# Attention products with v stored place by place innermost and summed by one reduction, and a new table of task places

## Chip, cores and metric

The kernel runs on one core of one Trainium2 chip. The metric is the device time of one execution in microseconds. Before the change three runs gave 622.37, 621.45 and 622.18 us; their median is 622.18 us. One more execution was profiled: its time was 621.86 us, and the profile's span (first to last instruction) is 620.1 us, so 1.76 us of that execution lie outside the span.

## What is computed

A token mixes two branches, attention with 32 heads over 8 places that lie 2 apart, and a Mish MLP, by a sigmoid gate:

```python
B, S, D = 1, 2048, 640; H = 32; Dh = 20; W, dil = 8, 2
idx = pos[:, None] - off[None, :]              # off = arange(8) * 2
logits = einsum("bhsd,bhswd->bhsw", q, kg) * scale    # masked where idx < 0
attn = softmax(logits, axis=-1)
o = einsum("bhsw,bhswd->bhsd", attn, vg)
a = o.reshape(B, S, D) @ wo
h = einsum("bsd,df->bsf", x, w1) + b1          # F = 1728
b = einsum("bsf,fd->bsd", h * tanh(softplus(h)), w2)
out = g * a + (1 - g) * b                      # g = sigmoid((x * gate_w).sum(-1))
```

The change touches the line that makes `o`.

## The kernel before

All matrix products run on TensorE (PE) with float32 inputs split into a high and a low part, so that each product is three matmuls (lines 481 to 483, function `mm3`). The split of a tile is made by two other engines: ScalarE (ACT) copies the high part (line 433), and VectorE (DVE) or GpSimd (POOL) subtracts it from the original to get the low part (line 436). The two parts lie in a `pair` tile, which PE reads. PE writes to seven PSUM banks.

The work is a list of tasks: `qkv` products for a quarter of the heads and half of the tokens at a time (eight units), `mlp1` and `quad` for the first MLP layer (a quad makes four blocks from seven products and hands partial sums from one bank to the next by ACT copies, line 927), `mlp2` for the second layer, and `wo_out` for the output product. The order of the products is given by the strings `FRONT` and `BACK`.

Attention itself is done by DVE. For each of the eight units there are four pieces of 2 x 128 tokens. In `scores` one multiplication of q with k for eight places (line 534, 2560 elements per partition) is followed by a reduction over the 20 features of a head (line 537). ACT has put q into the PSUM tile `side` before (line 540, task kind `qs`). In `outputs` the weights go to `side` (line 576), a multiplication with v (line 572) writes `pr` as [2 slots, 8 places, 160 features], and three additions halve the number of places: 8 to 4 (line 582), 4 to 2 (line 583), 2 to 1 into `q` (line 585).

The order of instructions on each engine is made when the program is built, by the class `Plan`: it plays the tasks through with a cost in ns each and takes, for an engine that is free, the task that is first by rank, due time and place in the list. Tasks of engine `ANY` (low parts and sums) go to POOL or DVE. While DVE is in a long instruction (`LARGE`: kinds `qk`, `qk sum`, `pv`), POOL may take a task that ends within it; while DVE is in any other instruction, POOL takes only tasks of rank below zero. Five tables correct single tasks by their number in the list: `MOVED` (place in the list), `HELD_BACK` (ready later), `NEEDED` (due time), `RANKED` (rank) and `ENGINE` (1 is DVE alone, 2 is POOL alone).

```python
LARGE, TOUCH = ("qk", "qk sum", "pv"), ("qk", "w", "pv")
...
if on and busy["DVE"]:
    fit = [t for t in fit if now + t.ns[0] <= quiet + 150 or t.rank < 0]
...
if t.kind in LARGE:
    begun = True
    quiet, gate = now + t.ns, last
```

DMAs of inputs, spills and results are issued by SyncE (SP); the sums of two MLP blocks are made by accumulating DMAs that POOL issues (line 723).

Of the kernel before, what the change touches and what calls it, by code (L numbers as in the profile page):

```python
# [11 lines left out]
OP = mybir.AluOpType  # L12
AX = mybir.AxisListType
# [3 lines left out]
S, D, H, DH, W, F = 2048, 640, 32, 20, 8, 1728  # L17
# [59 lines left out]

MOVED = """18:-4 500:-142 922:197 1244:301 1321:-2 1941:232"""  # L80
HELD_BACK = """110:1256 126:2874 359:1662 387:971 500:2708 581:193 635:839 703:214 822:16218 826:757 828:355 844:2726 848:5943
864:315 922:175 962:1932 963:501 1140:2261 1141:272 1142:308 1160:189 1243:1453 1246:859 1263:2549 1321:1969
1334:1062 1385:130 1756:782 1825:788 1862:478 2377:760 2413:1116 2426:2529"""
NEEDED = """110:-2061 119:-19498 126:21019 581:-1563 635:20514 822:-10954 828:12301 844:-408404 846:-3895 848:56321 931:-884144
937:33210 942:-278 962:3606 963:588 1140:661 1160:-787 1263:-714 1333:-255 1385:1390 1825:-252 1837:-186 2152:1905
2209:-17463 2413:1130 2426:-5153"""
RANKED = """80:0.25 822:-15.75 826:-1.25 828:-0.25 844:-10.25 848:-15.75 931:-119.25 937:-14 943:-1 1332:-1 1355:-1 1368:-1
1385:0.75 1753:-1 1837:0.25 1862:-1 2377:-0.25 2426:1"""
ENGINE = """119:2 846:2 1753:1 1756:1 1803:1 2128:2 2182:2 2252:1"""


class Plan:
# [36 lines left out]
    def run(self):  # L129
# [8 lines left out]
        touched = copied = None  # L138
        moved, held, needed, ranked, engine = map(table, (MOVED, HELD_BACK, NEEDED, RANKED, ENGINE))
        for i, t in enumerate(self.tasks):  # L140
# [144 lines left out]
def kernel(ctx: ExitStack, tc: tile.TileContext, x, wq, wo, w1, b1, w2, out):  # L285
    nc = tc.nc
    scale = DH ** -0.5
    V, G, A = nc.vector, nc.gpsimd, nc.scalar
# [112 lines left out]
    pw = side[:, :2 * W * HQ].rearrange("p (s w h) -> p s w h", w=W, h=HQ)  # L401
    qs = side[:, 2 * W * HQ:2 * W * HQ + 2 * QF].rearrange("p (s f) -> p s f", f=QF)
    pr = at.tile([128, 2, W, QF], F32, name="pr")
    mx = at.tile([128, 8, HQ], F32, name="mx")
    sm = at.tile([128, 8, HQ], F32, name="sm")

# [97 lines left out]
    def window(kv, s0, which):  # L504
        a = kv[:, s0:s0 + 9, which, :]
        return bass.AP(tensor=a.tensor, offset=a.offset, ap=[list(a.ap[0]), [ROW, 2], [ROW, W], [1, QF]])
# [7 lines left out]
    def attention(u, P, hq, ready, gates):  # L514


        kv, q = KV[UNIT[u]], Q[UNIT[u]]

        def turn_of(h, k):
            return LATER + 0.008 * (h + k / 7)  # L520

        def chain(rank):

            prev = [None]

            def step(eng, ns, fn, after=(), **k):
                prev[0] = add(eng, ns, fn, [prev[0]] + list(after), rank=rank if prev[0] is None else LATER - 0.5, **k)
                return prev[0]

            return step  # L530
# [30 lines left out]
        def shares(a, rank, after):  # L561
            h = slice(a, a + 4)
            step = chain(rank)
            step("DVE", 415, lambda: V.tensor_reduce(sm[:, h], lg[:, h], op=OP.add, axis=AX.X), after)
            step("DVE", 390, lambda: V.reciprocal(sm[:, h], sm[:, h]))
            return step("DVE", 230, lambda: V.tensor_tensor(sm[:, h], sm[:, h], gate[:, P, h, None].to_broadcast([128, 4, HQ]), op=OP.mult), gates)

        def outputs(s0, rank, after):
            def mul():
                vw = window(kv, s0, 1)  # L570
                vw = bass.AP(tensor=vw.tensor, offset=vw.offset, ap=[list(d) for d in vw.ap[:3]] + [[DH, HQ], [1, DH]])
                return V.tensor_tensor(pr.rearrange("p s w (h d) -> p s w h d", d=DH), vw,  # L572
                                       pw[:, :, :, :, None].to_broadcast([128, 2, W, HQ, DH]), op=OP.mult)

            def weights():
                return V.tensor_tensor(pw.rearrange("p s w h -> p s h w"), lg[:, s0:s0 + 2],  # L576
                                       sm[:, s0:s0 + 2, :, None].to_broadcast([128, 2, HQ, W]), op=OP.mult)

            step = chain(rank)
            step("DVE", 300, weights, after, kind="w")  # L580
            step("DVE", 2820, mul, kind="pv")
            step("DVE", 1495, lambda: V.tensor_tensor(pr[:, :, 0:4], pr[:, :, 0:4], pr[:, :, 4:8], op=OP.add))  # L582
            step("DVE", 855, lambda: V.tensor_tensor(pr[:, :, 0:2], pr[:, :, 0:2], pr[:, :, 2:4], op=OP.add))  # L583

            return step("DVE", 525, lambda: V.tensor_tensor(q[:, s0:s0 + 2], pr[:, :, 0], pr[:, :, 1], op=OP.add))

        def out(s0, rank, after):
            ot = plan.buf("ot", lambda: at.tile([128, QF // 32, 4, 32], F32, name="ot"))
# [8 lines left out]
        for i, a in enumerate((4, 0)):  # L597
            h = 2 * u + i
            t1 = scores(a + 2, turn_of(h - 1, 0), [shared_out.get(h - 2), prev])
            t2 = scores(a, turn_of(h - 1, 3), [t1])  # L600
            e = softmax(a, turn_of(h - 1, 6), [bounded(a, a + 4, [t1, t2])])
            w = shares(a, turn_of(h, 1), [e, shared_out.get(h - 2)])

            o = outputs(a + 2, turn_of(h, 2), [w, shared_out.get(h - 1)])
            o = outputs(a, turn_of(h, 4), [o])
            att_end[u] = out(a, turn_of(h, 5), [o])
            shared_out[h] = o
            prev = t2
# [859 lines left out]
```

## Time and profile before

| | busy us | share of span | instructions |
|---|---|---|---|
| PE matmuls | 614.4 | 99% | 2717 |
| DVE | 561.0 | 90% | 582 |
| ACT | 385.5 | 62% | 851 |
| POOL | 256.7 | 41% | 249 |

| | us |
|---|---|
| median of three runs | 622.18 |
| the profiled execution | 621.86 |
| its span | 620.1 |

A group of the profile names line, engine, operation and tiles with their shapes; `x32` is its count, then come the busy time, the mean ns of one, and the idle time of the engine just ahead of them. In a timeline a row gives the start, the length, the engine, the line, and in brackets how long the engine was idle ahead of it and what released it. Matmul records overlap, because matmuls are pipelined: a wait of PE is seen best in the distance between two starts.

### The profile page before, as it was taken

To read this page: it belongs to the slowest core of one execution; us is meant where nothing else is said; L and a number is where in the kernel's file an instruction comes from. 1 tells how busy PE (TensorE), PEld (TensorE's weight loads), DVE (VectorE), ACT (ScalarE), POOL (GpSimd) and SP (SyncE) were. 2 spreads that over 40 slices of the span, in tenths; PEclk is the share of its full clock that TensorE was granted. 3 is DMA by queue.
4 is the path that set the end of the run, shared out by engine and by line. 5 is a ranking of instruction groups with operands and counts; after the bars stand their busy time and mean duration, and the time that the engine had idled before them with its cause. 6 is when DMAs were issued, how large, how long until landed. Compare 5 with 4: busy or idle time off the path is not lost.

```text
span 620.1 us, 8931 instructions
## 1 busy us (share of the span) xinstructions
PE 614.4 (99%) x2717; PEld 509.3 (82%) x2717; DVE 561.0 (90%) x582; ACT 385.5 (62%) x851; POOL 256.7 (41%) x249
## 2 busy tenths in 40 slices
PE   9999999999999999999999999999999999999997
PEld 6888878887888888888888888888888888888885
DVE  5899999999999999999999999999899999999630
ACT  6765765766686677666676553556868356664234
POOL 2763267645464455445355665542013333303000
PEclk9999999999999999999999999999999999999999
DMA  8867289999999599989997999798987686965404
GB/s 308 260 197 209 86 251 267 287 252 243 322 258 283 150 319 298 232 235 271 265 259 212 315 265 263 214 274 287 347 278 255 214 274 215 284 212 175 135 1 170
DMA packets 100608, 149.46 MB, mean 241 GB/s; under 512 B 11456, under 2 KB 47296, under 8 KB 100528
## 3 DMA queue, kind: packets, MB, share of 16 engines
q1 hardware_dynamic: 93456, 136.05, 67.8%
q0 software_dynamic: 7104, 12.85, 13.1%
q8 instruction: 21, 0.34, 0.2%
q14 instruction: 27, 0.22, 0.1%
HBM read 85.61 MB, written 60.69 MB: 236 GB/s over the span
## 4 chain that ended last, share of the span: by engine, by line
PE 83%; DVE 11%; DMA 2%; issue 2%; ACT 1%; SPq 0%; POOL 0%; DVEq 0%; POOLq 0%; ACTq 0%
PE bank L481 27%; PE bank L483 27%; PE bank L482 27%; DVE pr L534 3%; DVE lg L537 2%; DMA raw<-in_x 2%; DVE pr L572 1%; DVE pair L436 1%; DVE pr L582 1%; DVE kvq L436 1%; PE bank L1248 1%; PE bank L1247 1%; DVE raw L780 0%; ACT L735 0%; SPq L442 0%
## 5 line engine op out<-in xcount | busy, mean ns | idle before, releaser
L482 PE MATMUL bank<-pair,pair 128*128 128x512 f32 (+2 forms) x812 | 314.5, 387 | 0.0
L483 PE MATMUL bank<-pair,pair 128*128 128x512 f32 (+2 forms) x812 | 314.4, 387 | 0.0
L481 PE MATMUL bank<-pair,pair 128*128 128x512 f32 (+2 forms) x812 | 314.2, 387 | 0.0
L436 POOL TENSOR_TENSOR pair<-raw,pair 128x512 fp32r<-128x512 f32 (+3 forms) x109 | 138.0, 1279 | 211.5 <-DVE side L576 39.0
L481 PEld LDWEIGHTS bank<-pair,pair 128*128 128x128 f32 x812 | 152.5, 188 | 30.2
L483 PEld LDWEIGHTS bank<-pair,pair 128*128 128x128 f32 x812 | 152.5, 188 | 30.1 <-POOL pair L436 0.2
L482 PEld LDWEIGHTS bank<-pair,pair 128*128 128x128 f32 x812 | 152.4, 188 | 30.1
L433 ACT ACTIVATE pair<-raw 128x512 fp32r<-128x512 f32 (+3 forms) x198 | 116.9, 610 | 32.7 <-DMA raw<-act 13.2
L572 DVE TENSOR_TENSOR pr<-kvq,side 128x2560 f32<-128x2560 f32 x32 | 90.2, 2820 | 1.0
L537 DVE TENSOR_REDUCE lg<-pr 128x128 f32<-128x2560 f32 x32 | 90.2, 2817 | 0.7
L534 DVE TENSOR_TENSOR pr<-kvq,side 128x2560 f32<-128x2560 f32 x32 | 90.0, 2812 | 0.4
L436 DVE TENSOR_TENSOR pair<-raw,pair 128x512 fp32r<-128x512 f32 (+4 forms) x89 | 58.5, 678 | 6.3 <-ACT pair L433 6.3
L633 ACT ACTIVATE kvq<-bank 128x320 f32<-128x320 f32 x64 | 27.9, 436 | 49.0 <-PE bank L483 48.5
L582 DVE TENSOR_TENSOR pr<-pr 128x1280 f32<-128x1280 f32 x32 | 47.7, 1490 | 0.7
L433 ACT ACTIVATE pair<-hb 128x512 fp32r<-128x512 f32 (+2 forms) x40 | 24.7, 618 | 15.3 <-DMA hb<-actt 7.7
L927 ACT ACTIVATE bank<-bank 128x512 f32<-128x512 f32 x36 | 21.0, 584 | 17.8 <-PE bank L483 17.5
L780 POOL TENSOR_TENSOR raw<-raw,raw 128x256 f32<-128x256 f32 (+1 forms) x20 | 20.6, 1034 | 25.7 <-DVE side L576 10.0
L481 PE MATMUL bank<-kvq,pair 128*128 128x512 f32 x72 | 28.3, 392 | 0.3 <-ACT bank L927 0.3
L723 POOL DMA_DIRECT2D actt<-actt x26 | 22.6, 881 | 13.5 <-DVE side L576 6.8
L483 PE MATMUL bank<-kvq,pair 128*128 128x512 f32 x72 | 28.1, 391 | 0.1
L482 PE MATMUL bank<-kvq,pair 128*128 128x512 f32 x72 | 28.0, 390 | 0.0
L583 DVE TENSOR_TENSOR pr<-pr 128x640 f32<-128x640 f32 x32 | 26.3, 823 | 0.8
(126 smaller groups left out, 583.4 us busy)
## 6 DMA issues: line engine op xcount, KB each, us to landing
raw<-in_w SPq DMA_DIRECT2D x34, 256.0 KB, 3.8
raw<-in_wq SPq DMA_DIRECT2D x30, 248.0 KB, 4.2
raw<-in_x SPq DMA_DIRECT2D x29, 256.0 KB, 5.3
raw<-actt SPq DMA_DIRECT2D x29, 256.0 KB, 4.5
actt<-hb SPq DMA_DIRECT2D x28, 256.0 KB, 3.4
act<-z SPq DMA_DIRECT2D x24, 256.0 KB, 4.4
actt<-z SPq DMA_DIRECT2D x24, 256.0 KB, 4.8
raw<-act SPq DMA_DIRECT2D x23, 256.0 KB, 3.9
```

What stands on the lines that cost most here:

```text
L433: a = add("ACT", act_ns(n), lambda: A.activation(hi(), raw(), AF.Copy), after, rank=rank, take=take, hold=hold, kind="hi")
L436: return (V if e == "DVE" else G).tensor_tensor(lo(), raw(), hi().bitcast(F32), op=OP.subtract)
L481: nc.tensor.matmul(ps, ah, bh, start=first, stop=False, skip_group_check=more)
L482: nc.tensor.matmul(ps, ah, bl, start=False, stop=False, skip_group_check=more)
L483: nc.tensor.matmul(ps, al, bh, start=False, stop=last, skip_group_check=more)
L534: return V.tensor_tensor(pr, window(kv, s0, 0), qs[:, :, None, :].to_broadcast([128, 2, W, QF]), op=OP.mult)
L537: return V.tensor_reduce(lg_w[:, s0:s0 + 2], pr.rearrange("p s w (h d) -> p s w h d", d=DH), op=OP.add, axis=AX.X)
L572: return V.tensor_tensor(pr.rearrange("p s w (h d) -> p s w h d", d=DH), vw, pw[:, :, :, :, None].to_broadcast([128, 2, W, HQ, DH]), op=OP ...
L582: step("DVE", 1495, lambda: V.tensor_tensor(pr[:, :, 0:4], pr[:, :, 0:4], pr[:, :, 4:8], op=OP.add))
L583: step("DVE", 855, lambda: V.tensor_tensor(pr[:, :, 0:2], pr[:, :, 0:2], pr[:, :, 2:4], op=OP.add))
L633: a = add("ACT", 330, lambda: A.activation(kv[:, 7 + s], ps.t[:, QF:3 * QF].rearrange("p (a b) -> p a b", a=2), AF.Copy), [done] + before, ...
L723: return add("POOL", 1200, lambda: G.dma_start(out=blk[key][:rows], in_=src(), accum_op=OP.add, max_dma_last_dim=2048), after, rank=-0.5, ...
```

## The change

The multiplication with v writes `pr` as [2 slots, 160 features, 8 places]: the same 2560 products, with the eight places of a feature side by side. One reduction over the innermost eight elements takes the place of the three additions. It carries the task kind `qk sum`, which is in `LARGE`, so that POOL may take tasks while it runs. Two tasks fewer for each of the 32 pieces shift the numbers of the task list, and the five tables are replaced: 173 tasks are named in them. The first line of two tables is shown; the rest is of the same kind.

```diff
-MOVED = """18:-4 500:-142 922:197 1244:301 1321:-2 1941:232"""
+MOVED = """3:-35739 474:-184 642:705 952:23 1073:18 1119:407 1589:110 2347:-102"""
...
-ENGINE = """119:2 846:2 1753:1 1756:1 1803:1 2128:2 2182:2 2252:1"""
+ENGINE = """105:2 609:2 787:2 798:2 804:2 814:2 822:1 824:2 1180:1 1344:2 1387:1 1431:1 1736:1 1765:1 1768:1 1787:1 1938:1
...
     pr = at.tile([128, 2, W, QF], F32, name="pr")
+
+    by_place = pr.rearrange("p s w f -> p (s w f)").rearrange("p (s f w) -> p s f w", s=2, w=W)
...
-                return V.tensor_tensor(pr.rearrange("p s w (h d) -> p s w h d", d=DH), vw,
+                return V.tensor_tensor(by_place.rearrange("p s (h d) w -> p s w h d", d=DH), vw,
                                        pw[:, :, :, :, None].to_broadcast([128, 2, W, HQ, DH]), op=OP.mult)
...
             step("DVE", 2820, mul, kind="pv")
-            step("DVE", 1495, lambda: V.tensor_tensor(pr[:, :, 0:4], pr[:, :, 0:4], pr[:, :, 4:8], op=OP.add))
-            step("DVE", 855, lambda: V.tensor_tensor(pr[:, :, 0:2], pr[:, :, 0:2], pr[:, :, 2:4], op=OP.add))
-
-            return step("DVE", 525, lambda: V.tensor_tensor(q[:, s0:s0 + 2], pr[:, :, 0], pr[:, :, 1], op=OP.add))
+            return step("DVE", 2820, lambda: V.tensor_reduce(q[:, s0:s0 + 2], by_place, op=OP.add, axis=AX.X), kind="qk sum")
```

On DVE the program has 582 instructions before and 474 after: 64 fewer by the reduction (32 pieces, three additions against one reduction), and 44 tasks that now stand on POOL, which goes from 249 to 293 computing and DMA instructions. ACT, PE and SP keep their counts. PE keeps its order except at two places: two neighbouring groups of 12 and 15 matmuls have changed places near its 1150th row, and three matmuls of the output product stand behind the last group of `mlp2` instead of within it.

Three places show what has moved. In the program of the change lines from 115 on have a number higher by 24 to 27: line 433 is 460, 436 is 463, 534 is 561, 537 is 564, 540 is 567, 559 is 586, 572 is 599, 576 is 603, 735 is 759, 738 is 762, 927 is 951, 960 is 984.

The first place is on ACT at the fifth quad: the rows ahead of the copy of a partial sum from one bank to another (the last row), for which PE waits. `hb` is a Mish result, `pair` a high part, `lg` the softmax. Before:

```order
L559 ACT_TABLE_LOAD
L559 ACTIVATE lg<-lg 128x256
L433 ACTIVATE pair_1549<-raw_1462 128x496
L433 ACTIVATE pair_1551<-raw_1483 128x512
L433 ACTIVATE pair_1554<-raw_1485 128x128
L735 ACT_TABLE_LOAD
L735 ACTIVATE hb_1562<-bank_65,bias 128x512
L927 ACTIVATE bank_63<-bank_66 128x512
```

After, on the same engine at the same place:

```order
L586 ACT_TABLE_LOAD
L586 ACTIVATE lg<-lg 128x256
L460 ACTIVATE pair_1546<-raw_1378 128x512
L759 ACT_TABLE_LOAD
L759 ACTIVATE hb_1554<-bank_65,bias 128x512
L762 ACTIVATE hb_1554<-hb_1554 128x512
L951 ACTIVATE bank_69<-bank_66 128x512
```

Two high parts have left the place between the softmax and the table load, and the sign change of the Mish result (line 738, now 762) has come ahead of the copy.

The second place is on DVE about half way, ahead of a low part (the last row) that PE waits for. Before:

```order
L537 TENSOR_REDUCE lg<-pr 128x2x8x8
L564 TENSOR_REDUCE sm<-lg 128x32
L565 RECIPROCAL sm<-sm 128x32
L566 TENSOR_TENSOR sm<-sm,gate 128x32
L576 TENSOR_TENSOR side<-lg,sm 128x2x8x8
L572 TENSOR_TENSOR pr<-kvq_220,side 128x2560
L582 TENSOR_TENSOR pr<-pr 128x2x640
L583 TENSOR_TENSOR pr<-pr 128x2x320
L436 TENSOR_TENSOR pair_3034<-raw_2768,pair_3034 128x512
```

After, up to the low part for the same matmul:

```order
L564 TENSOR_REDUCE lg<-pr 128x2x8x8
L591 TENSOR_REDUCE sm<-lg 128x32
L463 TENSOR_TENSOR pair_2931<-raw_2638,pair_2931 128x512
L592 RECIPROCAL sm<-sm 128x32
L593 TENSOR_TENSOR sm<-sm,gate 128x32
L603 TENSOR_TENSOR side<-lg,sm 128x2x8x8
L599 TENSOR_TENSOR pr<-kvq_220,side 128x2x8x160
L609 TENSOR_REDUCE kvq_220<-pr 128x320
L463 TENSOR_TENSOR pair_3003<-raw_2715,pair_3003 128x512
```

The low part now stands behind the whole reduction instead of behind two of the three additions, and another low part, which was POOL's, stands a little ahead of it. Between the program's start and this place ten low parts and sums have left DVE and two have come.

The third place is on ACT at the seventh quad, the first of the second half of the tokens: again the last row is a copy for which PE waits. `side` is the copy of q for the next scores. Before:

```order
L540 ACTIVATE side<-kvq_221 128x320
L433 ACTIVATE pair_2194<-raw_2044 128x512
L433 ACTIVATE pair_2196<-raw_2104 128x512
L433 ACTIVATE pair_2201<-raw_2165 128x512
L735 ACTIVATE hb_2216<-bank_67,bias 128x512
L927 ACTIVATE bank_66<-bank_65 128x512
```

After:

```order
L460 ACTIVATE pair_2186<-raw_2090 128x512
L659 ACTIVATE kvq_220<-bank_63 128x160
L661 ACTIVATE hx<-bank_63 128x16
L759 ACTIVATE hb_2199<-bank_65,bias 128x512
L762 ACTIVATE hb_2199<-hb_2199 128x512
L567 ACTIVATE side<-kvq_221 128x320
L951 ACTIVATE bank_69<-bank_64 128x512
```

The next piece's copy into `side`, which waits for a product of DVE, has come to stand directly ahead of the bank copy.

More of the change, by code (lines that the diff above doesn't have):

```diff
@@ L75, in table @@
     return {int(k): float(v) for k, v in (x.split(":") for x in text.split())}
-MOVED = """18:-4 500:-142 922:197 1244:301 1321:-2 1941:232"""
[L81 to L88, printed above, removed]
-ENGINE = """119:2 846:2 1753:1 1756:1 1803:1 2128:2 2182:2 2252:1"""
+MOVED = """3:-35739 474:-184 642:705 952:23 1073:18 1119:407 1589:110 2347:-102"""
+HELD_BACK = """47:1772 105:2796 194:249 206:4982 275:2229 280:2031 332:748 347:1872 359:14775 410:1130 474:268 549:194 586:2291
[8 rows of a table added]
+2347:1033 2354:3770 2361:3137 2396:3376 2432:1854 2577:1744"""
+NEEDED = """47:-2237 105:4534 194:14591 267:-4437 275:-5217 280:3361 332:1122 347:6591 359:40694 410:1237 549:-1053 585:-2486
[10 rows of a table added]
+2332:2818 2349:4494 2354:917 2396:1972 2397:6400 2433:9557 2441:-21260 2443:-6928 2512:171"""
+RANKED = """105:-2 194:1 206:0.75 267:-0.25 280:-1 332:0.25 347:1.75 359:-8.75 410:1.25 458:-1.25 549:2 585:-1.75 586:-1.25
[8 rows of a table added]
+2314:-0.25 2332:1.25 2345:-0.25 2349:-1 2354:1 2355:-1 2361:-1 2377:1.25 2432:-1 2433:1 2441:-1 2443:-1"""
+ENGINE = """105:2 609:2 787:2 798:2 804:2 814:2 822:1 824:2 1180:1 1344:2 1387:1 1431:1 1736:1 1765:1 1768:1 1787:1 1938:1
+1979:2 1991:2 2056:2 2061:1 2145:2 2191:1 2224:2 2230:2 2264:1 2281:1 2295:2 2314:1 2396:2 2397:2 2433:2 2512:2"""
 class Plan:
```

26 rows, old and new, of tables (HELD_BACK, NEEDED, RANKED) are left out of this document.

## The prediction

> **What bounds the kernel now.** I read the page's first and fourth parts, then who PE waits for, then PE's timeline at the waits, then stretches.
>
> ```profile
> PE 614.4 (99%) x2717; PEld 509.3 (82%) x2717; DVE 561.0 (90%) x582; ACT 385.5 (62%) x851; POOL 256.7 (41%) x249
> ...
> PE 83%; DVE 11%; DMA 2%; issue 2%; ACT 1%; SPq 0%; POOL 0%; DVEq 0%; POOLq 0%; ACTq 0%
> ```
>
> PE is busy for 614.4 of 620.1 us, 614.4 / 2717 = 0.226 us for a matmul, and the change neither removes nor shortens one. So whatever DVE and POOL gain, the most that can go is what PE waits. The view of waits, for PE alone, has two rows, and the second hides more than it says, since overlapping records cover most of a wait. The timeline of PE shows the three places where two starts are further apart than 0.226 us:
>
> ```profile
> PE bank L416 <- DVE lg L412: 1.2, 1, 1.2
> PE bank L481 <- ACT bank L927: 0.3, 2, 0.2
> ```
>
> ```profile
> 80.56 0.39 PE L483 MATMUL bank<-kvq,pair 128*128 128x512 f32 x1
> 81.12 0.50 PE L481 MATMUL bank<-kvq,pair 128*128 128x512 f32 x1 [0.18 <-ACT bank L927]
> 81.46 0.40 PE L482 MATMUL bank<-kvq,pair 128*128 128x512 f32 x1
> ...
> 144.19 0.39 PE L483 MATMUL bank<-kvq,pair 128*128 128x512 f32 x1
> 144.75 0.50 PE L481 MATMUL bank<-kvq,pair 128*128 128x512 f32 x1 [0.17 <-ACT bank L927]
> 145.08 0.40 PE L482 MATMUL bank<-kvq,pair 128*128 128x512 f32 x1
> ...
> 304.07 0.39 PE L482 MATMUL bank<-kvq,pair 128*128 128x512 f32 x1
> 304.51 0.50 PE L483 MATMUL bank<-kvq,pair 128*128 128x512 f32 x1
> 304.84 0.39 PE L481 MATMUL bank<-kvq,pair 128*128 128x512 f32 x1
> ```
>
> Over the two steps shown PE should need 0.45 us. It needs 0.90, 0.89 and 0.77: lost are **0.45, 0.44 and 0.32 us**, 1.21 in all. Ahead of PE's stream stands the load of the first tiles, behind it one copy and the last store:
>
> ```profile
> 616.10 0.60 ACT L1321 ACTIVATE kvq<-bank 128x512 f32<-128x512 f32 x1 [0.82 <-PE bank L483]
> ```
>
> Both ends are made of the same instructions after the change. So the floor is 1.21 us under today's time. The stretches show why so little is lost and why it is fragile:
>
> ```profile
> 0.00:40.00 40.00, 38.80 (x164) 30.34 (x165) 30.98 (x35) 27.47 (x71) 20.76 (x20) 1.00 0.82 270
> 40.00:160.00 120.00, 119.65 (x533) 99.59 (x532) 116.47 (x101) 79.20 (x177) 62.10 (x65) 1.00 0.82 230
> ...
> 280.00:400.00 120.00, 119.95 (x538) 100.68 (x537) 116.89 (x105) 70.24 (x173) 66.14 (x67) 1.00 0.91 259
> ...
> 500.00:580.00 80.00, 80.00 (x354) 66.25 (x353) 77.08 (x101) 45.65 (x89) 21.32 (x18) 1.00 0.72 231
> 580.00:620.00 40.00, 36.00 (x159) 29.47 (x157) 9.26 (x14) 13.61 (x24) 0.00 (x0) 0.99 0.26 92
> ```
>
> The columns are PE, weight loads, DVE, ACT, POOL. DVE is at 96 to 97% from 40 to 580 us: a second engine just below its limit, feeding the first in time. PE's granted clock is 1.00, so nothing is to be had there.
>
> **The change, part by part.** The rows that price it:
>
> ```profile
> L572 DVE TENSOR_TENSOR pr<-kvq,side 128x2560 f32<-128x2560 f32 x32 | 90.2, 2820 | 1.0
> L537 DVE TENSOR_REDUCE lg<-pr 128x128 f32<-128x2560 f32 x32 | 90.2, 2817 | 0.7
> L582 DVE TENSOR_TENSOR pr<-pr 128x1280 f32<-128x1280 f32 x32 | 47.7, 1490 | 0.7
> L436 DVE TENSOR_TENSOR pair<-raw,pair 128x512 fp32r<-128x512 f32 x68 | 45.6, 685 | 5.5 <-ACT pair L433 5.5
> L583 DVE TENSOR_TENSOR pr<-pr 128x640 f32<-128x640 f32 x32 | 26.3, 823 | 0.8
> L585 DVE TENSOR_TENSOR kvq<-pr 128x320 f32<-128x320 f32 x32 | 15.7, 490 | 0.9
> L576 DVE TENSOR_TENSOR side<-lg,sm 128x128 f32<-128x128 f32 x32 | 9.7, 302 | 1.6 <-ACT side L540 0.6
> L558 DVE TENSOR_TENSOR lg<-lg,mx 128x256 f32<-128x256 f32 x16 | 6.8, 423 | 0.4
> L557 DVE TENSOR_REDUCE mx<-lg 128x32 f32<-128x256 f32 x16 | 6.3, 391 | 0.0
> ```
>
> *The reduction.* Gone are 1490 + 823 + 490 = 2803 ns for each of 32 pieces. The new one reads 2560 elements by eights. L557 reduces by eights too (391 ns for 256), L537 by twenties (2817 for 2560): the line through both has 1.053 ns an element and no sign of a price for each sum written. I take 2.82 us: 32 x 0.015 = 0.5 us more busy time on DVE, against some 1.6 us less of gaps (0.7 + 0.8 + 0.9 before three instructions, one remains). **Nothing** within what DVE can notice.
>
> *The strided products.* The multiplication now steps 32 bytes from one product to the next. No row writes SBUF so. L576 writes PSUM with that step: 302 ns for 128 elements, where L558 (423 for 256, side by side) less 128 x 1.053 gives 288. That is 14 ns, 0.11 an element, at most 0.28 us for 2560 and 9 us for 32. I take nothing, because most of the 14 ns may be PSUM's, and keep 9 us as the upper end; below nothing I see no end, since 2820 ns is already one element a step. The Trainium skill (SBUF — State Buffer, Door 1: The DMA port swizzle) says SBUF has lines of 16 bytes and each access that crosses to a new one pays a penalty, so that fp32 may step four elements for free; eight is past that, and by it the sum would be the first rival's below. No run here shows it yet.
>
> *Forty-four tasks go to POOL.* Off DVE: 44 x 0.685 = 30 us. On POOL, by this row, 44 x 1.317 = 58 us, 257 to 315 of 620:
>
> ```profile
> L436 POOL TENSOR_TENSOR pair<-raw,pair 128x512 fp32r<-128x512 f32 x75 | 97.8, 1317 | 167.8 <-DVE side L576 35.0 <-DVE pair L436 33.2 <-DVE lg L558 30.5
> ```
>
> POOL sat idle 168 us ahead of those tasks, and the 32 reductions open 90 us more to it. A task alone ends 0.6 us later than on DVE. Even with the 9 us of strided writes DVE has 21 us less to do, so the cover holds.
>
> *The copy at 144 us.* It is hidden by nothing: ACT runs late there.
>
> ```profile
> 141.89 0.31 ACT L433 ACTIVATE pair<-raw 128x128 fp32r<-128x128 f32 x1 [0.59 <-PE bank L483]
> 142.22 1.28 ACT L735 ACT_TABLE_LOAD   x1
> 143.52 0.69 ACT L735 ACTIVATE hb<-bank,bias 128x512 f32<-128x512 f32 x1
> 144.10 0.59 ACT L927 ACTIVATE bank<-bank 128x512 f32<-128x512 f32 x1
> ```
>
> The first place shown in the order has the 128x128 high part, ahead of which ACT sat idle 0.59 us, and one more high part out of the way. The table load can follow the other high part, which ends no later than about 141.3 (141.89 less that 0.59): 141.3 + 1.28 + 0.69 + 0.61 for the sign change less two overlaps of 0.1 is 143.7, where the copy now starts at 144.10. That gains 0.4 of the 0.44 us. **I take -0.44**; if the softmax ahead comes later by half a microsecond, nothing.
>
> *The low part at 304 us.* Before, it comes behind two additions:
>
> ```profile
> 301.50 1.49 DVE L582 TENSOR_TENSOR pr<-pr 128x1280 f32<-128x1280 f32 x1
> 303.02 0.83 DVE L583 TENSOR_TENSOR pr<-pr 128x640 f32<-128x640 f32 x1
> 303.77 1.29 DVE L436 TENSOR_TENSOR pair<-raw,pair 128x512 fp32r<-128x512 f32 x2
> ```
>
> After, it stands behind the whole reduction, 0.49 us more. Up to there eight tasks net have left DVE, 8 x 0.685 = 5.5 us; 17 pieces with 0.015 more take 0.3. DVE can be there 4.7 us sooner, and needs 0.4. **I take -0.32**; what is late next is the copy behind it, ready in its turn.
>
> *The copy at 81 us.* In both orders these stand ahead of it in the same succession, and DVE's work up to there is the same but for additions against reductions:
>
> ```profile
> 78.14 0.44 ACT L540 ACTIVATE side<-kvq 128x320 f32<-128x320 f32 x1 [0.97 <-DVE pr L534]
> 78.60 1.28 ACT L735 ACT_TABLE_LOAD   x1
> ```
>
> **0**: its 0.45 us stay. DMAs are the same transfers; their order on SP follows the buffers, POOL's 50 accumulating DMAs stand between more of its tasks. I put **0** for this, with the third rival as its price.
>
> Sum against the profiled execution: 621.86 - 0.44 - 0.32 = 621.1. The median is 0.32 above that execution, so 622.18 - 0.76 = **621.4 us**.
>
> **The rivals.**
>
> *1. Strided writes at half rate: slower.* If every product takes two steps, a multiplication grows by 2560 x 1.053 = 2.7 us, 32 of them by 86 us. DVE's slack: 620.1 - 561.0 = 59, of which 30.7 lie in the last 40 us and 9 in the first 40, unusable; 19 remain, and 30 are freed. 86 - 49 = 37 us: **659 us**. It decides from 49 / 32 = 1.5 us a multiplication. For it stands only the page named above; against it L576's 14 ns. 4%.
>
> *2. New waits of PE: slower.* ACT copies a partial sum while PE has six matmuls to do, 6 x 0.226 = 1.36 us. A copy that is not kept back leaves little:
>
> ```profile
> 215.06 0.58 ACT L927 ACTIVATE bank<-bank 128x512 f32<-128x512 f32 x1 [0.69 <-PE bank L483]
> ...
> 217.60 2.80 DVE L534 TENSOR_TENSOR pr<-kvq,side 128x2560 f32<-128x2560 f32 x1
> ```
>
> PE's next use is 0.6 us behind its end. In the third place of the order the copy into `side` now stands directly ahead, and waits for the multiplication that ends at 220.40 before. ACT and PE behind it stand still until that ends. By the order DVE has by then 13 low parts and sums fewer ahead of it, 13 x 0.685 = 9 us, so that it can end near 211 and the copy is safe by over 3 us. Past that point every microsecond of delay is PE's, up to a product's 2.8 us. The same price holds for any of the 44 low parts held behind one DVE product of 2.8 us. With one such wait more than what is gained: 621.4 + 2.8 = **624.2 us**. Against it: DVE's load falls and POOL has room. For it: 173 tasks stand elsewhere, and margins are tenths of a microsecond. 25%.
>
> *3. The change shifts nothing at the three waits.* The gain on DVE becomes idle time, and the three waits stay, or come again elsewhere in the same size, with 0.0 to 0.8 us more by late DMAs: **622.4 us**. 27%.
>
> *4. Everything late goes.* All 1.21 us and a few tenths at the start: **620.8**. 6%.
>
> **How the numbers follow.** My forecast (621.4, give or take 0.5) has 38%; the rivals have 4, 25, 27 and 6%. A measurement of this kernel tells some 0.2%, 1.24 us, from no change: the bounds are 620.94 and 623.42. Faster: rival 4 and a little of the forecast, 10%. Same: the rest of the forecast, rival 3 and a small part of rival 2, 65%. Slower: 25%. The range from 620.7 to 624.4 takes in the forecast, rival 3 and rival 2 with one wait; several waits at once and rival 1 are left out.
>
> **What will show it.** The product with v at 2.8 us and its reduction at 2.8 us (rival 1: 5.5). DVE busy near 530 us, POOL near 315, PE 614 still. In PE's starts no gap near 144 and 304 us and one of 0.45 at 81; a new gap over 1 us behind a bank copy or a POOL low part is rival 2. I am wrong if PE's gaps sum to over 2.5 us or the span falls below 618.5.

## The result, and the profile after

| | us | span of the profiled execution |
|---|---|---|
| before, 4 runs beside the change | 622.02 (621.45 to 622.37) | 620.1 |
| the change, 4 runs | 682.60 (681.70 to 684.14) | 680.9 |
| ratio | 1.098, 95% interval 1.096 to 1.100 | |

The change makes the kernel 61 us slower. The forecast was 621.4, and its range ended at 624.4.

The page of the changed kernel (its first, second and fourth parts) shows at once that PE is no longer the engine that sets the pace: busy for 93% of the span where it was 99%, with single slices of granted clock below full, and with 22% of the final chain where it had 83%.

```profile
span 680.9 us, 8944 instructions
PE 635.2 (93%) x2717; PEld 518.3 (76%) x2717; DVE 619.5 (91%) x474; ACT 385.0 (57%) x851; POOL 315.6 (46%) x293
PEclk9999899989999989999999989989989998999999
PE 22%; DVE 10%; issue 5%; DMA 3%; POOL 2%; ACT 1%; POOLq 1%; SPq 1%; DVEq 0%; ACTq 0%
```

DVE has 58.5 us more to do (619.5 against 561.0). The groups by line say which instruction brings it; the columns are count, busy us, mean ns of one, and idle us ahead:

```profile
L599 DVE TENSOR_TENSOR pr<-kvq,side 128x2560 f32<-128x2560 f32 x32 | 164.0, 5124 | 0.9
L609 DVE TENSOR_REDUCE kvq<-pr 128x320 f32<-128x2560 f32 x32 | 90.1, 2816 | 0.8
L463 DVE TENSOR_TENSOR pair<-raw,pair 128x512 fp32r<-128x512 f32 x56 | 43.2, 782 | 3.3 <-ACT pair L460 3.3
L463 POOL TENSOR_TENSOR pair<-raw,pair 128x512 fp32r<-128x512 f32 x87 | 113.7, 1315 | 117.1 <-DVE side L603 18.2 <-DVE pr L599 12.9 <-PE bank L510 12.5
```

The product with v takes 5124 ns where it took 2820: 32 x 2.304 = 73.7 us more. The reduction takes 2816 ns, 32 x 0.013 = 0.4 us more in all than the three additions. The moved tasks therefore took only 73.7 + 0.4 - 58.5 = 15.6 us off DVE. Its low parts of 512 elements are twelve fewer, but in the mean each takes 782 ns where it took 685: by the records the 40 with no GpSimd instruction in their time took 681 ns, the 16 others 1037.

One row of the windows for each kernel puts this beside the rest. The columns are start and end, length, PE, weight loads, DVE, ACT, POOL (busy us, instructions), clock, DMA share, GB/s; this is before, from 40 to 580 us:

```profile
40.00:580.00 540.00, 539.60 (x2397) 449.51 (x2396) 520.77 (x535) 344.41 (x758) 235.93 (x230) 1.00 0.85 250
```

And the change, the same stretch and the rest:

```profile
40.00:580.00 540.00, 500.96 (x2140) 409.49 (x2139) 532.84 (x375) 310.53 (x698) 275.34 (x262) 0.97 0.80 229
580.00:700.00 120.00, 95.44 (x420) 78.38 (x418) 53.36 (x66) 45.87 (x83) 20.34 (x11) 0.99 0.38 127
```

DVE was idle for 19.2 of these 540 us before and is idle for 7.2 now. In this stretch PE does 257 matmuls fewer. The second engine has become the first.

The five largest waits of PE in the change (us in total, times, longest), where before there were two rows with 1.5 us:

```profile
PE bank L510 <- DVE pair L463: 14.2, 4, 4.7
PE bank L508 <- ACT hx L661: 9.4, 8, 2.9
PE bank L509 <- DVE pair L463: 6.7, 4, 2.4
PE bank L508 <- ACT pair L460: 4.3, 1, 4.3
PE bank L508 <- ACT bank L951: 3.6, 2, 2.0
```

Only part of them names DVE. That DVE can stand behind a row of ACT too shows at one of the two waits for a bank copy. The timeline of DVE ahead of it (start, length):

```profile
66.43 2.82 DVE L609 TENSOR_REDUCE kvq<-pr 128x320 f32<-128x2560 f32 x1
69.17 0.29 DVE L603 TENSOR_TENSOR side<-lg,sm 128x128 f32<-128x128 f32 x1
69.49 5.10 DVE L599 TENSOR_TENSOR pr<-kvq,side 128x2560 f32<-128x2560 f32 x1
```

The timeline of ACT, whose copy into `side` has to wait for that product to end at 74.59, with all that is queued behind it:

```profile
74.62 0.44 ACT L567 ACTIVATE side<-kvq 128x320 f32<-128x320 f32 x1 [2.53 <-DVE pr L599]
75.00 0.60 ACT L460 ACTIVATE pair<-raw 128x496 fp32r<-128x496 f32 x1
75.51 0.16 ACT L661 ACTIVATE hx<-bank 128x16 f32<-128x16 f32 x1
75.69 1.28 ACT L759 ACT_TABLE_LOAD   x1
76.99 0.69 ACT L759 ACTIVATE hb<-bank,bias 128x512 f32<-128x512 f32 x1
77.58 0.59 ACT L951 ACTIVATE bank<-bank 128x512 f32<-128x512 f32 x1
```

The timeline of PE, which waits for the last of these:

```profile
75.81 0.39 PE L510 MATMUL bank<-pair,pair 128*128 128x512 f32 x1
78.22 0.50 PE L508 MATMUL bank<-pair,pair 128*128 128x512 f32 x1 [2.02 <-ACT bank L951]
78.56 0.46 PE L509 MATMUL bank<-pair,pair 128*128 128x512 f32 x1
78.81 0.63 PE L510 MATMUL bank<-pair,pair 128*128 128x512 f32 x1
79.23 0.63 PE L508 MATMUL bank<-pair,pair 128*128 128x512 f32 x1
...
81.79 0.57 PE L508 MATMUL bank<-pair,pair 128*128 128x512 f32 x1
82.20 0.40 PE L509 MATMUL bank<-pair,pair 128*128 128x512 f32 x1
```

The wait is paid twice. Two starts are 2.41 us apart, and then the starts come every 0.427 us instead of every 0.226 us until 82.2: PE runs at half its clock (the granted clock is 0.50 from 78.8 to 82.1 us). The distances between the starts of all matmuls behind the kernel's start-up give the whole loss: 28 waits of 46.2 us, 55 matmuls at half clock that lose 11 us, and smaller gaps of 3 us, in all 60 us. Before, the same sum is 1.2 us.

### The profile page after: what moved, and what is told of

The parts are those of the page before. It is cut to its first block, busy times and chain, and to the rows that moved or that the text cites. A ratio compares the mean times of both kernels' runs of the same rounds, so it can differ in the third digit from the quotient of the medians.

```text
span 680.9 us, 8944 instructions
## 1 busy us (share of the span) xinstructions
PE 635.2 (93%) x2717; PEld 518.3 (76%) x2717; DVE 619.5 (91%) x474; ACT 385.0 (57%) x851; POOL 315.6 (46%) x293
## 5 line engine op out<-in xcount | busy, mean ns | idle before, releaser
L508 PE MATMUL bank<-pair,pair 128*128 128x512 f32 (+2 forms) x812 | 319.2, 393 | 17.1 <-ACT hx L661 9.4
L509 PE MATMUL bank<-pair,pair 128*128 128x512 f32 (+2 forms) x812 | 318.6, 392 | 6.7 <-DVE pair L463 6.7
L510 PE MATMUL bank<-pair,pair 128*128 128x512 f32 (+2 forms) x812 | 318.4, 392 | 6.6 <-DVE pair L463 5.8
L463 POOL TENSOR_TENSOR pair<-raw,pair 128x512 fp32r<-128x512 f32 (+4 forms) x123 | 156.3, 1282 | 166.3 <-ACT pair L460 29.5
L508 PEld LDWEIGHTS bank<-pair,pair 128*128 128x128 f32 x812 | 154.8, 191 | 52.7 <-ACT hx L661 13.2
L509 PEld LDWEIGHTS bank<-pair,pair 128*128 128x128 f32 x812 | 154.6, 190 | 39.3 <-DVE pair L463 9.0
L510 PEld LDWEIGHTS bank<-pair,pair 128*128 128x128 f32 x812 | 154.7, 191 | 38.5 <-DVE pair L463 6.6
L599 DVE TENSOR_TENSOR pr<-kvq,side 128x2560 f32<-128x2560 f32 x32 | 164.0, 5124 | 0.9
L609 DVE TENSOR_REDUCE kvq<-pr 128x320 f32<-128x2560 f32 x32 | 90.1, 2816 | 0.8
L564 DVE TENSOR_REDUCE lg<-pr 128x128 f32<-128x2560 f32 x32 | 90.1, 2815 | 0.7
L561 DVE TENSOR_TENSOR pr<-kvq,side 128x2560 f32<-128x2560 f32 x32 | 90.0, 2811 | 0.5
L463 DVE TENSOR_TENSOR pair<-raw,pair 128x512 fp32r<-128x512 f32 (+4 forms) x75 | 56.8, 775 | 3.6 <-ACT pair L460 3.5
L567 ACT ACTIVATE side<-kvq 128x320 f32<-128x320 f32 x32 | 14.1, 442 | 46.3 <-DVE pr L561 43.7
L510 PE MATMUL bank<-kvq,pair 128*128 128x512 f32 x72 | 30.4, 423 | 8.4 <-DVE pair L463 8.4
L508 PE MATMUL bank<-kvq,pair 128*128 128x512 f32 x72 | 30.2, 419 | 1.6 <-ACT bank L951 1.6
L463 DVE TENSOR_TENSOR pair<-hb,pair 128x512 fp32r<-128x512 f32 (+2 forms) x22 | 14.7, 671 | 17.7 <-ACT pair L460 17.7
L509 PE MATMUL bank<-kvq,pair 128*128 128x512 f32 x72 | 29.9, 415 | 0.0
L804 POOL TENSOR_TENSOR raw<-raw,raw 128x256 f32<-128x256 f32 (+1 forms) x23 | 22.0, 964 | 16.5 <-DVE side L603 5.6
```

The lines of the kernel that those rows point to most:

```text
L463: return (V if e == "DVE" else G).tensor_tensor(lo(), raw(), hi().bitcast(F32), op=OP.subtract)
L508: nc.tensor.matmul(ps, ah, bh, start=first, stop=False, skip_group_check=more)
L509: nc.tensor.matmul(ps, ah, bl, start=False, stop=False, skip_group_check=more)
L510: nc.tensor.matmul(ps, al, bh, start=False, stop=last, skip_group_check=more)
L561: return V.tensor_tensor(pr, window(kv, s0, 0), qs[:, :, None, :].to_broadcast([128, 2, W, QF]), op=OP.mult)
L564: return V.tensor_reduce(lg_w[:, s0:s0 + 2], pr.rearrange("p s w (h d) -> p s w h d", d=DH), op=OP.add, axis=AX.X)
```

## The experiments

Three theories stood after the result: that only writing by steps is slow (W), that reading by steps is slow as well, so that any layout pays once (R), and that GpSimd beside DVE makes both slower (C). Times are medians beside runs of the kernel before, which gave 621.85 to 622.0 on the three chips. A kernel with one run has no interval.

### The layout alone, in the order of before

The program and the tables of before, with the stepped product; the three additions become three reductions of about the same lengths, so that the task numbers fit. To match the lengths, this kernel leaves out the sums of 37 of the 160 features of one slot.

```diff
-                return V.tensor_tensor(pr.rearrange("p s w (h d) -> p s w h d", d=DH), vw,
+                return V.tensor_tensor(by_place.rearrange("p s (h d) w -> p s w h d", d=DH), vw,
...
+            step("DVE", 1495, lambda: V.tensor_reduce(q[:, s0], by_place[:, 0], op=OP.add, axis=AX.X))
+            step("DVE", 855, lambda: V.tensor_reduce(q[:, s0 + 1, :80], by_place[:, 1, :80], op=OP.add, axis=AX.X))
...
+            return step("DVE", 525, lambda: V.tensor_reduce(q[:, s0 + 1, 80:123], by_place[:, 1, 80:123], op=OP.add, axis=AX.X))
```

> The kernel before with its order and tables, and the change's layout alone: the strided product, and the reduction in three tasks of about 1.49, 0.80 and 0.48 us in the places of the three additions; the sums of 37 of 160 features of one of the two slots are left out so that the lengths match. Theory W: product 5.12 us, 74 us more on VectorE with at most 19 us of slack to take it, time 680 to 700 us. Rival P: the layout costs little in this order, time under 650 us.

One run: 673.19 us, 51 more than before. The groups by line:

```profile
L574 DVE TENSOR_TENSOR pr<-kvq,side 128x2560 f32<-128x2560 f32 x32 | 163.9, 5123 | 1.0
L584 DVE TENSOR_REDUCE kvq<-pr 128x160 f32<-128x1280 f32 x32 | 47.4, 1482 | 0.8
```

The layout by itself brings the 5.12 us and most of the loss, with none of the 173 tasks moved and POOL as free as before. It is less than the 680 to 700 us that were expected: of 73.7 us the old order loses 51, the new one 61. Both orders were made for a product of 2.82 us; one made for 5.12 us was not tried.

### The lengths that the prediction assumed, in the order of the change

The product is written side by side as before, and the reduction still reads eight neighbours, which are now eight features of a place. Both instructions then have the lengths of the forecast, and everything else is the change.

```diff
-                return V.tensor_tensor(by_place.rearrange("p s (h d) w -> p s w h d", d=DH), vw,
+                return V.tensor_tensor(pr.rearrange("p s w (h d) -> p s w h d", d=DH), vw,
```

> The change's order, tables and task kinds, with the product written side by side as before the change and the reduction reading eight neighbours, so that nothing steps: the sums are of eight features of a place instead of the eight places of a feature. These are the lengths that the forecast took (2.82 and 2.82 us). Theory W2 (the whole loss comes from the stepped access and what its length does to an order planned for 2.82 us): 621.4 us as forecast, 620.9 to 622.4. Rival P (the new placement has a loss of its own): over 624 us.

Ten runs: 621.14 us (620.70 to 622.44), ratio 0.9989 [0.9980, 0.9998]. The groups by line:

```profile
L599 DVE TENSOR_TENSOR pr<-kvq,side 128x2560 f32<-128x2560 f32 x32 | 90.2, 2818 | 0.9
L609 DVE TENSOR_REDUCE kvq<-pr 128x320 f32<-128x2560 f32 x32 | 90.1, 2816 | 0.8
```

And all waits of PE:

```profile
PE bank L443 <- DVE lg L439: 1.2, 1, 1.2
PE bank L509 <- DVE pair L463: 0.6, 1, 0.6
```

The first is the start-up, the second a new one at 428 us. So the placement of the 173 tasks loses nothing in sum, and with the lengths of the forecast its sum comes out (621.4 against 621.14). That it fits so closely is luck in part: by PE's starts the wait at 81 us, which was to keep its 0.45 us, is gone as well, and the new one costs 0.9. All 61 us hang on one length.

### The three additions in one task

The product as before, and the three additions issued one behind the other in the one task that the change has for the reduction: the change's order without its layout.

```diff
+            def adds():
+                V.tensor_tensor(pr[:, :, 0:4], pr[:, :, 0:4], pr[:, :, 4:8], op=OP.add)
+                V.tensor_tensor(pr[:, :, 0:2], pr[:, :, 0:2], pr[:, :, 2:4], op=OP.add)
+                return V.tensor_tensor(q[:, s0:s0 + 2], pr[:, :, 0], pr[:, :, 1], op=OP.add)
...
-            return step("DVE", 2820, lambda: V.tensor_reduce(q[:, s0:s0 + 2], by_place, op=OP.add, axis=AX.X), kind="qk sum")
+            return step("DVE", 2820, adds, kind="qk sum")
```

> The layout and the three additions of before, as one task of the change's order, with GpSimd beside it as the change lets it. Theory W: product 2.82 us, the additions 2.8 us where GpSimd is idle, time within 2 us of e1. Rival C (VectorE instructions with two SBUF inputs and GpSimd beside them hold each other up): the additions 10% or more over 2.80 us in sum, GpSimd's low parts over 1.4 us, time 5 to 20 us over e1.

Four runs: 652.92 us (651.32 to 660.45), ratio 1.053 [1.046, 1.059]. The groups by line:

```profile
L603 DVE TENSOR_TENSOR pr<-pr 128x1280 f32<-128x1280 f32 x32 | 48.2, 1505 | 0.8
L604 DVE TENSOR_TENSOR pr<-pr 128x640 f32<-128x640 f32 x32 | 49.3, 1541 | 1.1
L605 DVE TENSOR_TENSOR kvq<-pr 128x320 f32<-128x320 f32 x32 | 32.4, 1012 | 1.1
L463 POOL TENSOR_TENSOR pair<-raw,pair 128x512 fp32r<-128x512 f32 x87 | 129.4, 1495 | 92.8 <-ACT bank L956 14.3 <-DVE lg L585 14.0 <-DVE pair L463 9.2
```

The second and third addition take about twice what they took before (823 and 490 ns), and a low part on POOL takes 1495 ns instead of 1317. Theory C holds for the additions: with GpSimd at work beside them 2803 ns become 4058. The records of the two engines show it one by one. An addition that begins while GpSimd is in no instruction keeps its length, even if GpSimd begins one during it: 30 first ones took 1489 ns in the mean, 5 second ones 825, 12 third ones 492. One that begins while GpSimd is in an instruction is longer: 27 second ones took 1674 ns in the mean, 20 third ones 1324, and they end 0.68 and 0.35 us behind the end of that instruction, whatever their length; of the two first ones of this kind one took 2017 ns. So what begins second waits, and the first addition keeps its length because it nearly always begins first.

It does not hold for the reduction, which reads one tensor and took 2815 to 2822 ns beside the same GpSimd tasks in every run of this order in which it reads neighbours. The Trainium skill (GPSIMD Engine Reference, Specifications) names DVE instructions with two inputs in SBUF among those that contend with GpSimd; the two doubled additions agree. So replacing the additions by a reduction is what makes room for POOL. The kernel's time was expected against that of the next experiment, which came out otherwise itself, so only the lengths can be held against the expectation.

### Reading by steps instead of writing by steps

The product is written as before, and the reduction steps over the places, 160 elements or 640 bytes from one to the next.

```diff
-                return V.tensor_tensor(by_place.rearrange("p s (h d) w -> p s w h d", d=DH), vw,
+                return V.tensor_tensor(pr.rearrange("p s w (h d) -> p s w h d", d=DH), vw,
...
-            return step("DVE", 2820, lambda: V.tensor_reduce(q[:, s0:s0 + 2], by_place, op=OP.add, axis=AX.X), kind="qk sum")
+            return step("DVE", 2820, lambda: V.tensor_reduce(q[:, s0:s0 + 2], pr.rearrange("p s w f -> p s f w"), op=OP.add, axis=AX.X), kind="qk sum")
```

> The product with v writes pr as before the change (features innermost, side by side); the one reduction reads the eight places of a feature 160 elements apart. Order, tables and task kinds are the change's. Theory W (a write that steps 32 bytes takes nearly two steps an element, a read does not): product 2.82 us, reduction 2.82 us, time 621 to 624 us. Rival R (any access with such a step is slow): product 2.82, reduction about 5.1 us, time near 682 us. Rival P (it is the placement of the 173 tasks): product 2.82, time still over 640 us.

Four runs: 674.47 us (674.05 to 674.60), ratio 1.085 [1.083, 1.086]. The groups by line:

```profile
L609 DVE TENSOR_REDUCE kvq<-pr 128x320 f32<-128x2560 f32 x32 | 157.0, 4907 | 0.8
L599 DVE TENSOR_TENSOR pr<-kvq,side 128x2560 f32<-128x2560 f32 x32 | 90.2, 2819 | 0.9
```

The product is back at 2819 ns, and the reduction has gone to 4907. Theory W falls: reading by steps costs nearly as much.

The second kernel of this kind keeps the layout of the change, but lets the multiplication run over the places innermost: it writes side by side and reads v in steps of 1280 bytes. The weights in `side` (in PSUM) are laid out for it, so that line 603 now writes them side by side where it wrote them 32 bytes apart.

```diff
-    pw = side[:, :2 * W * HQ].rearrange("p (s w h) -> p s w h", w=W, h=HQ)
+    pw = side[:, :2 * W * HQ].rearrange("p (s h w) -> p s w h", w=W, h=HQ)
...
-                return V.tensor_tensor(by_place.rearrange("p s (h d) w -> p s w h d", d=DH), vw,
+                return V.tensor_tensor(by_place.rearrange("p s (h d) w -> p s h d w", d=DH), vw,
```

> The product with v runs over the places first, so that it writes pr in the change's layout side by side; now v is read with a step of 1280 bytes, and the weights lie in PSUM with the places side by side. The reduction is the change's. Theory W: product 2.8 to 2.9 us, time 621 to 624 us. Rival R: product about 5.1 us or more, time near 682 us.

One run: 675.87 us. The groups by line:

```profile
L599 DVE TENSOR_TENSOR pr<-kvq,side 128x2560 f32<-128x2560 f32 x32 | 154.9, 4840 | 0.9
...
L603 DVE TENSOR_TENSOR side<-lg,sm 128x128 f32<-128x128 f32 x32 | 9.7, 304 | 1.0
```

Reading v by steps costs the product 4840 ns. The second row settles something else: the weights cost 304 ns side by side, and 302 (before) to 319 (the change) with the 32-byte step. These means differ by the few that ran beside GpSimd: the 27 of 32 with no GpSimd instruction in their time took 295 ns side by side and 296 in both kernels with the step. The step in PSUM costs this instruction nothing, and its row was the one from which the prediction took its price for a step in SBUF.

### Shorter steps

The products of k places stand beside each other, in `pr` as [slot, 8/k groups, feature, k places]; k is 2, 4, 8, 4 for successive units (four pieces each), so that steps of 8, 16 and 32 bytes are measured in one run. The reduction runs over the two innermost dimensions.

```diff
+            k = (2, 4, 8, 4)[u % 4]
+            flat = pr.rearrange("p s w f -> p (s w f)")
...
+                return (flat.rearrange("p (s c h d w) -> p s c w h d", s=2, c=W // k, d=DH, w=k), vw,
...
+                by = flat.rearrange("p (s c f w) -> p s f c w", s=2, c=W // k, w=k)
...
+                    return V.tensor_reduce(q[:, s0:s0 + 2], by, op=OP.add, axis=AX.XY)
```

> The change with pr as [slot, 8/k, feature, k places], so that the products are written with a step of k elements and the sums read k neighbours at a time; k is 2, 4, 8, 4 by unit, one source line for each. Theory L (two accesses in a 16-byte piece are enough): k = 2 (8 bytes) takes 2.82 us written and read, k = 4 (16 bytes) takes 4.8 to 5.1 written and 2.82 read, k = 8 takes 5.12 and 2.82. Rival S (any step but 1 costs): k = 2 takes about 5 us written. Rival G (the price grows with the step): k = 2 about 3.4, k = 4 about 4 us. Time 640 to 675 us.

One run: 660.19 us. The groups by line, 8, 16 and 32 bytes in this order, then the reduction for 8:

```profile
L608 DVE TENSOR_TENSOR pr<-kvq,side 128x2560 f32<-128x2560 f32 x8 | 22.5, 2818 | 0.2
...
L610 DVE TENSOR_TENSOR pr<-kvq,side 128x2560 f32<-128x2560 f32 x16 | 76.3, 4766 | 0.5
...
L612 DVE TENSOR_TENSOR pr<-kvq,side 128x2560 f32<-128x2560 f32 x8 | 41.0, 5121 | 0.2
...
L617 DVE TENSOR_REDUCE kvq<-pr 128x320 f32<-128x2560 f32 x8 | 22.5, 2818 | 0.2
```

A step of 8 bytes is free, one of 16 bytes costs 1.95 us, one of 32 bytes 2.30. The reduction for 8 reads two neighbours and then jumps 1280 bytes to the next pair, and that is free too. Both fit pieces of 16 bytes, in which two accesses are enough for full speed. A step of 12 bytes was not tried.

### Pairs of places, and fours

The same code with k = 2 in all pieces keeps the reduction, the order and the sums of the change; the products are written 8 bytes apart, and the reduction reads them in pairs of neighbours.

```diff
-            k = (2, 4, 8, 4)[u % 4]
+            k = (2,)[u % 1]
```

> k = 2 in all units: pr as [slot, 4, feature, 2 places], right sums. Theory L: product 2.82, reduction 2.82, time as e5, 621 to 622.5 us, and so level with the kernel before. Rival S: product about 5 us, near 680 us.

Ten runs: 620.99 us (620.39 to 622.40), ratio 0.9984 [0.9974, 0.9993]. Its page, first part:

```profile
PE 614.3 (99%) x2717; PEld 510.5 (82%) x2717; DVE 550.4 (89%) x474; ACT 384.4 (62%) x851; POOL 311.4 (50%) x293
```

Its groups by line, the product and DVE's low parts:

```profile
L608 DVE TENSOR_TENSOR pr<-kvq,side 128x2560 f32<-128x2560 f32 x32 | 90.2, 2820 | 0.9
...
L463 DVE TENSOR_TENSOR pair<-raw,pair 128x512 fp32r<-128x512 f32 x56 | 45.1, 818 | 5.9 <-ACT pair L460 5.7
```

Its row of the windows, to be held against the two above:

```profile
40.00:580.00 540.00, 540.00 (x2404) 451.02 (x2403) 508.45 (x428) 343.44 (x759) 290.83 (x274) 1.00 0.86 251
```

PE is busy for all of the 540 us and waits for nothing behind its start. This version is faster than the change, and than the kernel before by 0.16%, which is near the limit of what ten runs can tell (the interval ends at 0.9993). With k = 4 instead:

> k = 4 in all units: pr as [slot, 2, feature, 4 places], right sums. Theory L: product 4.8 to 5.1 us, reduction 2.82, time 672 to 683 us. Rival G: product about 4 us, near 650 us.

One run: 671.91 us, the product at 4769 ns. Most of the loss, 50.9 of 61.6 us, lies between a step of two elements and one of four.

### Pairs of places in the order of before

The layout in pairs, with the program and tables of before and three reductions as in the first experiment, which leave out the same sums.

> The kernel before, its order and tables, with pairs of places and the reduction in three tasks of 1.49, 0.80 and 0.48 us in the places of the three additions (the sums of 37 of 160 features of one slot are left out, as in e4). Theory O (e7's gain on before is the new placement, which takes PE's three waits away): 622.0 us, 621.5 to 622.6, with the waits near 80, 144 and 304 us still there. Rival Q (the reduction itself, one input where the additions had two, frees the time): 620.5 to 621.3 us and the waits gone.

Ten runs: 621.50 us (620.90 to 622.20), ratio 0.9993 [0.9983, 1.0002]. PE still waits for the bank copy at the fifth quad:

```profile
144.50 0.39 PE L485 MATMUL bank<-kvq,pair 128*128 128x512 f32 x1
145.07 0.50 PE L483 MATMUL bank<-kvq,pair 128*128 128x512 f32 x1 [0.17 <-ACT bank L933]
```

0.57 instead of 0.226 us: this wait goes with the placement, not with the reduction. Of the other two, which were expected to stay as well, the one at 81 us is gone and the one at 304 us is down to 0.19 from 0.32 us, so neither expectation holds in full. In whole times the two can't be told apart: 0.9984 with the new order and 0.9993 with the old one have overlapping intervals, so how much of the 0.16% belongs to which stays open.

### Length alone

Is it the length of the product that costs 61 us, or does writing by steps do harm beside that? The pairs of places again, with one more multiplication of 1920 elements ahead of each product, in the same task, without any long step (its results are written over by the product).

```diff
+                V.tensor_tensor(to[:, :, :, :, :6], v[:, :, :, :, :6], p[:, :, :, :, :6], op=OP.mult)
                 if k == 2:
                     return V.tensor_tensor(to, v, p, op=OP.mult)
```

> e7 (pairs of places, nothing at full price) with one more instruction ahead of each product: the same products for six of the eight heads, written twice, 1920 elements, about 2.15 us. Theory W3 (what costs is the length on VectorE; time = 621 + 32 x extra length - some 12 us of slack, as the other runs of this order give it): 32 x 2.18 = 70, so 679 us, 675 to 683. Rival M (slow accesses cost the other engines something of their own): under 665 us, since nothing here steps.

One run: 690.08 us. The groups by line:

```profile
L607 DVE TENSOR_TENSOR pr<-kvq,side 128x1920 f32<-128x1920 f32 x32 | 68.9, 2153 | 0.9
```

68.9 us more on DVE cost 69 us, so no harm by the step itself is needed to explain the change. The number was missed all the same: it is 7 us above the upper end. The distances between PE's starts say where: 75 matmuls run at half clock here and lose 15 us, against 11 us in the change, and the waits are 50.4 us against 46.2. The price of a length isn't a straight line, as the kernels side by side show, each against the 620.99 us of the pairs of places (the chips differ by at most 0.2 us in the kernel before):

| kernel, in the order of the change | added to DVE, us | lost, us |
|---|---|---|
| steps of 8, 16, 32 bytes mixed | 16 x 1.95 + 8 x 2.30 = 49.6 | 39.2 |
| 16 bytes throughout | 32 x 1.95 = 62.4 | 50.9 |
| v read by 1280 bytes | 32 x 2.02 = 64.6 | 54.9 |
| reduction reads by 640 bytes | 32 x 2.09 = 66.9 | 53.5 |
| length alone | 68.9 | 69.1 |
| the change, 32 bytes | 73.7 | 61.6 |

## Why the prediction was wrong

**What bounds the kernel.** The reading was right: PE, with DVE just below its limit from 40 to 580 us (96% in the mean, though 94% from 400 to 500 us, where "96 to 97%" was said), and 1.21 us as all that could be gained. In pairs of places PE waits for nothing between its start and its end, and 620.99 us is 1.0 under the 622.0 beside it.

**The strided products: the step that failed.** "I take nothing" a multiplication, "at most 0.28 us", and the runs show 2.30. The row behind it, L576, steps 32 bytes, but it writes PSUM; the kernel with its weights side by side shows that PSUM asks nothing for the step there. So the row was no witness for SBUF, and the upper end taken from it was no bound. The prediction said that no row writes SBUF so, and then let the row from the other memory set its range. One row does write SBUF 32 bytes apart: L537 puts its sums into `lg` with that step. It took 2817 ns all the same, but it writes one sum for 20 elements that it reads, and so says nothing of a step at every element. An honest upper end for an unseen access was the rival's, twice the time. The Trainium skill's rule (SBUF — State Buffer, Door 1: The DMA port swizzle) was right in its direction, and its two accesses for each 16-byte line agree with the free step of 8 bytes; its "4 fp32", read in the prediction as a step of four elements, does not agree: the 16-byte step takes 4.77 us against 2.82.

**The first rival was the mechanism, and came out too low:** 659 us for 682.6. Its terms were 86 us of price less 30 freed and 19 of slack. The price is 73.7, so 12 less. Freed are 15.6, so 14 more of a loss. Of the slack of 19 us DVE's idle time shows 12 used, 7 more. And PE's half clock, for which it had no term, loses 11. That makes 20 of the 24 us missing; this is an account, not a test of each part, and the rest is not assigned. "It decides from 1.5 us a multiplication" is wrong with it: in the table the loss is never more than 13.4 us short of the added length, so that, if it runs straight down from there, it begins at 13.4 us or less, about 0.4 us a multiplication. No run tried so short a length.

**The reduction.** 2.82 us was said, 2816 ns measured, and no price for each sum written, as the line through two rows had it. That it replaces additions at 2803 ns holds only as long as POOL stays where it was: beside the change's POOL tasks they take 4058 ns.

**Forty-four tasks to POOL.** POOL's 315 us were right (315.6; 311.4 in pairs of places). "30 us off DVE" was mis-sized: DVE's busy time fell by 561.0 - 550.4 = 10.6 us where the product kept its length, since what was left on DVE got slower beside a busier POOL. In the records the tasks that left are worth 30 us by their lengths before, as forecast; but what stayed there beside the products and their sums takes 14 us longer in all (the rest of the difference is overlap of records, which the busy time counts once). Twelve fewer low parts of 512 elements save almost nothing: 68 with a mean of 685 ns kept DVE busy for 45.6 us, 56 with a mean of 818 ns for 45.1. Of these 56 the 44 with no GpSimd instruction in their time took 681 ns, the 12 others 1319.

**The three waits.** The copy at 144 us and the low part at 304 us lose their waits in both kernels with the lengths of the forecast, as the order said (-0.44 and -0.32); at 144 us the old order keeps its wait. The copy at 81 us was to keep its 0.45 us and is in time in those two and in the old order with pairs. In the two executions with pairs PE reaches its 340th matmul 0.8 us later than in the one before, and with the lengths of the forecast 0.5 us later; its clock is full from 7.1, 6.9 and 6.4 us on, where it was from 5.1 before. So the matmuls at half clock in the start-up are more, and the start's loss and this wait seem to stand in for each other. That is one execution each, and was not tested.

**The other rivals.** The second had its mechanism in the change: the copy into `side` directly ahead of ACT's work holds PE up behind a product, as at 74.62 us, but only because that product is long; with the lengths of the forecast it costs nothing. The fourth (all waits go, 620.8) is what pairs of places do. What was to show it did: a product above 5 us, DVE at 619.5 where 530 was said, and PE's gaps far over 2.5 us.

## What to carry to other kernels

Before a layout is turned so that one reduction fits, count the bytes from one element to the next in every SBUF access of DVE, writes and reads: for fp32 a step of two elements was free here and one of four or more at every element cost 1.7 to 1.8 times the time, and pairs gave the same single reduction for nothing. A price for an access is taken from a row of the same memory, or its range stays as wide as the worst rule known. And a second engine at 96% has almost no slack: of what was added to it in the table about four fifths or more went on to the time, PE's half clock included.

## What the runs showed of the hardware

- **Steps in SBUF, on DVE, 2560 fp32 elements.** Written: 2.82 us side by side, 2.82 by 8 bytes, 4.77 by 16, 5.12 by 32. Read: 4.91 by 640 bytes (reduction), 4.84 by 1280 (product). Read in pairs of neighbours 1280 bytes apart (reduction): 2.82. In PSUM 128 elements, with no GpSimd instruction beside them, took 296 ns written by 32 bytes and 295 side by side.
- **DVE beside GpSimd.** An addition of two SBUF tensors that began while GpSimd was in an instruction ended behind it: 1674 ns for 640 elements and 1324 for 320 in the mean, against 825 and 492 without. One that began first kept its time (1489 ns for 1280 elements), and so did the reduction, with one input (2816).
- **PE's clock.** Behind gaps of about 2 to 6 us between two starts, not behind every one, the matmuls start 0.427 us apart at a granted clock of 0.50, in the records for stretches of 3.41 or 6.83 us (once, in the layout alone, behind two gaps of 1.1 and 1.4 us). The Trainium skill (TensorE: Matmul & The Clock Gate, What's actually happening) gives a window of 3.4 us that runs freely, and half rate after at least one idle window: the lengths of the stretches agree, but here a gap of 2.41 us between two starts was enough.
